# A routed feed-forward kernel: weight copies, the last weight split, the logits' update and the levels of the expert search put at other places in the schedule

## The chip, the cores and the metric

The kernel runs on one core of one Trainium2 chip. The metric is the device time of one execution in microseconds (us), taken as the median of several runs. The core has five engines that each work through their own instruction stream in order: TensorE (PE) for matrix products, VectorE (DVE), ScalarE (ACT), GpSimd (POOL) and SyncE (SP), which here only issues transfers. They wait for each other through semaphores.

## The reference

A gated linear attention produces 3072 rows of 384 numbers, and a mixture of 8 experts with a fixed capacity works on these rows. What is left of the second part when it is cut to what matters:

```python
logits = x @ w_gate                       # 3072 x 8
order = np.argsort(-logits.flatten())
for idx in order:                         # greedy, best score first
    tok, e = idx // E, idx % E
    if assigned[tok] >= 0 or counts[e] >= cap: continue      # cap = 384
    assigned[tok] = e; counts[e] += 1
for e in range(E):
    mask = assigned == e
    out[mask] = np.maximum(x[mask] @ w1[e], 0.0) @ w2[e]     # 384 -> 1024 -> 384
```

## The kernel before, in words

The first part of the span, up to about 150 us, computes the attention and the logits; nothing of it is touched. The rest treats the experts in the order in which they fill up, and does two things at once.

**The products.** For every expert, PE works through 8 blocks `q` of 128 hidden features. `ffn1(i, q)` (L818) is 9 matmuls into a PSUM tile `h`, of which there are two; ACT then writes `hh` (L823, the rounded ReLU) and DVE `hl` (L824, what the rounding left). `ffn2(i, q)` (L838) is 9 matmuls into `y`. Both use weights that are split into a rounded part and a residual: `split_hi` (L771, L772) is two copies on ACT into `whi`, `split_lo` (L780) two subtractions on POOL into `wlo`, so 16 subtractions `n` = 0 to 15 for an expert. The rows of the next expert are turned on PE (`rows`, L800), copied by ACT (`xh`, L801), and their residual `xl` is taken on DVE (`rows_lo`, L806). An expert has 144 product matmuls, and all 8 experts' products stand in one row, which sets the positions of everything else.

**The search.** While the products run, the kernel finds which expert fills up next and at which score. One search has five levels `t` = 0 to 4. Each level is a ring through two engines: PE counts (`counts`, L600, 24 small matmuls with the table `cmp` as weights), DVE compares with what room is left (`g`, L605), PE spreads that over the partitions (`flags`, L586, one matmul), DVE takes the level's digit (`k`, L588), the next digit (`nd`, L592) and builds the next table (`cmp`, L547), which the next level's counts wait for. After the fifth level `find` (L614 to L626) names the expert and starts the first half of its weights; `offsets` on PE and `places` on DVE (L644 to L675) give every chosen token its place, `one_hot` (L682, L684) turns the places into the tables `hot` and `rhs`, and PE multiplies them into a list of indices (`index`, L691). DVE copies it (`idx`, L696), POOL issues three gathers of the expert's rows (L698), and `best_left` (L720 to L735) strikes the full expert out of the logits `L`, takes every token's best score `m` that is left, and so begins the next search. The second half of the expert's weights is issued behind the gathers.

**What sets the order.** The order is written out by hand: `at(position, step)` puts a step before the product matmul of that number, and all instructions of a step go to the ends of their engines' streams at that moment. A loop over `i` places one search per round: round `i` holds the search for expert `i + 1` and the splits of expert `i`. A round's positions are counted from its `base`; `offs` holds the places of the five levels, `end` the place of the index matmuls, from which the next round's `base` follows. A step that has a small position difference to another leaves little time for the engines to go round. `BEHIND` gives for each of the 16 subtractions the level whose table must have been built first (0 to 4); this is an added wait on POOL, so that subtractions do not run while DVE builds a table.

In this text "search 2" is round `i` = 1 and "searches 3 to 6" are rounds 2 to 5, which have the same positions. Search 7 (round 6) is a shorter one. Expert 1's search lies in front of the loop, and is not touched.

Of the kernel before, what the change touches and what calls it, by code (L numbers as in the profile page):

```python
# [11 lines left out]
F16 = mybir.dt.float16  # L12
ROUTE_AHEAD = 3
LAST_BLOCKS = 2
BEHIND = (0, 0, 0, 1, 1, 2, 2, 3, 3, 4, 4, 4, 4, 4, 4, 4)
FREE_LAST = 4
WARM_UP = 10
Y_IN_LEVEL = (None, 11, 8, 8, 8)
# [8 lines left out]
OP = mybir.AluOpType  # L27
# [3 lines left out]
def gla_moe_kernel(ctx, tc, q, k, v, alpha, w_gate, w1, w2, out):  # L31
# [487 lines left out]
    def col(x, n=NU):  # L519
        return x[:, None, :].to_broadcast([128, n, x.shape[-1]])  # L520
# [157 lines left out]
    def one_hot(i):  # L678
        hot = st["hot"] = rw.tile([128, NW, T, U], F16, name="hot", bufs=1)
        rhs = st["rhs"] = rw.tile([128, NU, NB], F16, name="rhs")  # L680
        for a, js in enumerate(halves(i)):
            x = nc.vector.tensor_tensor(words(hot, T, js), keyed(st["wb"], T, js), each(iota, T, js), op=OP.is_equal)  # L682
            if a == 0:
                nc.vector.tensor_tensor(rhs, st["bk"], row(cst_c, NB), op=OP.mult)  # L684
        if i == E - 1:
            compared[i] = [None] * FREE_LAST + [x]

    def index(i):
        ix = psx.tile([128, NB], F32, name="xt")
# [27 lines left out]

    def best_left(i):
        es, v = st["es"], st["v"]
        nc.vector.scalar_tensor_tensor(L, col(cl_c), BIGNEG, L, op0=OP.mult, op1=OP.add)  # L720
        nc.vector.tensor_reduce(m_c, L, axis=X, op=OP.max)
        nc.vector.scalar_tensor_tensor(sel_c, v, float(CAP), qe_c, op0=OP.is_le, op1=OP.mult)
        val = st["val"] = rw.tile([128, NU, E], BF, name="val")
        if i + 2 < E:
# [50 lines left out]
    def split_lo(i, n):  # L775
        q, h = divmod(n, 2)
        if (i, q) not in CH:
            return False
        hi, lo, x = CH[i, q]
        y = nc.gpsimd.tensor_sub(lo[:, h], x[h], hi[:, h])  # L780
        if i + 1 in compared:
            after = compared[i + 1][BEHIND[n] if i + 2 < E else min(n, FREE_LAST)]
            if after is not None:
                tc.add_manual_dep(y.ins, after.ins.name,
                                  mybir.DependencyInfo(mybir.DependencyClass.Sync, mybir.DependencyReason.DATA),
                                  reason="weights split while the search reads one table at a time")
# [96 lines left out]
    def at(pos, fn, *args):  # L883
        plan.append((pos, len(plan), fn, args))
# [76 lines left out]
        at(p, split_lo, 0, n)  # L961
    base = 90
    for i in range(1, E):
        offs = dict(enumerate((36, 51, 65, 79, 93)))
        end = 140 if i == 1 else 144
        renewed(base, i) if i < E - 1 else at(base, gather, i)
        if i < E - 1:
            at(base + 9, new_choice, i)
        if i < E - 2:
            at(base + 14, table, i + 1, 0)  # L970
            at(base + 14, left, i)
        for b, p in enumerate((25, 34, 41) if i < E - 1 else (45, 60, 75)):
            at(base + p, rows, i, b)
        if i < E - 2:
            levels(base, i + 1, offs, {0: (0, 1), 1: (2,)})
            found(base + offs[4] + 3, i + 1, end - offs[4] - 3)
        else:
            for b, p in enumerate((29, 38, 45) if i < E - 1 else (49, 64, 79)):
                at(base + p, rows_lo, i, b)
        if i == E - 2:  # L980
            at(base + 12, find_last, i + 1)
# [3 lines left out]
            end = 58  # L985
            at(base + end, index, i + 1)
        if i < E - 2:
            hi = (24, 32, 50, 64, 86, 98, 108, 118)
            lo = (26, 26, 32, 55, 55, 71, 71, 87, 87, 103, 103, 103, 108, 108, 118, 118)
        elif i == E - 2:  # L990
            hi = (24, 32, 50, 64, 80, 96, 106, 118)
            lo = (26, 27, 32, 33, 50, 51, 64, 65, 80, 81, 96, 97, 106, 107, 118, 119)
        else:
            hi = [80 + 18 * q for q in range(5)] + [160, 170, 206]
            lo = [x for p in hi for x in (p, p + 1)]
# [70 lines left out]
```

## Time and profile before

| what | value |
|---|---|
| median of 3 runs (lowest, highest) | 425.96 us (425.06, 426.38) |
| the profiled execution's own time | 424.76 us |
| its span from first to last instruction | 423.1 us |
| mean granted clock of TensorE | 0.978 |
| PE busy | 394.1 us, 93% of the span |
| DVE busy | 288.8 us, 68% |
| POOL busy | 268.3 us, 63% |
| ACT busy | 194.0 us, 46% |
| bytes moved by DMA | 63.40 MB, mean 150 GB/s |

The durations in the prediction come from the profiled execution. Its time is 1.66 us more than its span, for what lies around it, and 1.20 us less than the median of the runs. PE is the engine that is nearly always busy, so the questions to put to this profile are where PE stands idle after the attention, for whom, and whether those waits go or come. A row of the timeline has the start and the duration in us, the engine, the line, the operation with its tiles, and in brackets how long the engine sat idle before it and who ended that. PE's matmuls overlap: the record of a product matmul is 0.33 us long, but the next one starts 0.17 us later. So what a wait costs PE is read from start to start.

### The profile page before, as it was taken

Reading aid. Unit: us, or ns where it says so; the run is one execution under the profiler, and the core shown is the slowest. Engines: PE = TensorE matmul, PEld = TensorE weight load, DVE = VectorE, ACT = ScalarE, POOL = GpSimd, SP = SyncE. Lnnn points to the kernel's source line nnn. Section 1 sums busy time; section 2 is a strip of 40 time slices with the busy share of each in tenths; the row PEclk is TensorE's granted clock in tenths of the full one; section 3 lists DMA queues with packets and bytes.
Section 4 is the critical chain, followed back from the end, with each engine's and each line's share of the span. In section 5 each row is a group of like instructions: output and inputs, shape, how many; then the busy total and the mean of one; then the engine's idle time right before and its main releaser. Section 6 shows DMA issues by size and latency. Waiting matters only on the chain.

```text
span 423.1 us, 10874 instructions
## 1 busy us (share of the span) xinstructions
PE 394.1 (93%) x4151; PEld 345.5 (82%) x4151; DVE 288.8 (68%) x836; ACT 194.0 (46%) x447; POOL 268.3 (63%) x327
## 2 busy tenths in 40 slices
PE   7999999889898958999999999999999999999993
PEld 3787777677676637998899899899899899999993
DVE  8888787888745686697697688589578677521220
ACT  2477566566575523425325325424343443654511
POOL 4668978677730026646566765665785775799932
PEclk9699999999999989999999999999999999999997
DMA  8999997670004577054055145155153333961011
GB/s 289 320 253 242 243 253 221 179 203 28 2 2 151 196 221 240 21 185 150 4 185 167 58 160 195 39 170 177 66 169 106 139 120 106 338 221 58 5 53 57
DMA packets 34884, 63.40 MB, mean 150 GB/s; under 512 B 3360, under 2 KB 15392, under 8 KB 34832
## 3 DMA queue, kind: packets, MB, share of 16 engines
q1 hardware_dynamic: 28592, 48.54, 37.9%
q0 software_dynamic: 3072, 9.44, 6.9%
q10 hardware_dynamic: 3168, 4.72, 3.2%
q8 instruction: 33, 0.54, 0.5%
q14 instruction: 19, 0.16, 0.1%
HBM read 53.25 MB, written 9.44 MB: 148 GB/s over the span
## 4 chain that ended last, share of the span: by engine, by line
PE 69%; DVE 17%; issue 4%; POOL 3%; ACT 3%; DMA 1%; DVEq 0%; ACTq 0%; POOLq 0%
PE y L838 18%; PE h L818 18%; PE rt L600 6%; PE y L314 5%; PE y L308 5%; PE s L259 5%; DVE hot L682 3%; DVE cmp L547 3%; PE xt L251 3%; POOL wlo L780 2%; PE st L327 2%; PE st L281 2%; DVE sc L222 2%; PE xt L691 2%; DVE ga L227 2%
## 5 line engine op out<-in xcount | busy, mean ns | idle before, releaser
L780 POOL TENSOR_TENSOR wlo<-w1r,whi 128x384 fp32r<-128x384 f32 x64 | 64.9, 1015 | 30.6 <-ACT whi L771 13.7
L823 ACT ACTIVATE hh<-h 128x384 fp32r<-128x384 f32 x64 | 31.5, 492 | 114.8 <-PE h L818 105.9
L780 POOL TENSOR_TENSOR wlo<-w2r,whi 128x384 fp32r<-128x384 f32 x64 | 66.4, 1037 | 20.7 <-DVE cmp L547 13.2
L824 DVE SCALAR_TENSOR_TENSOR hl<-h,hh 128x384 fp32r<-128x384 f32 x64 | 35.4, 553 | 46.8 <-ACT hh L823 45.7
L838 PE MATMUL y<-whi,hl 128*128 128x384 f32 x192 | 66.6, 347 | 0.0
L838 PE MATMUL y<-wlo,hh 128*128 128x384 f32 x192 | 65.8, 342 | 0.0
L838 PE MATMUL y<-whi,hh 128*128 128x384 f32 x192 | 65.3, 340 | 0.0
L698 POOL DMA_INDIRECT xr<-x_dram,idx x24 | 23.2, 966 | 51.4 <-DVE asg L728 29.3
L271 POOL TENSOR_SCALAR_AFFINE_SELECT sm<-sm 128x512 f32<-128x512 f32 x48 | 29.4, 639 | 31.5 <-ACT sm L267 31.5
L818 PE MATMUL h<-xh,whi 128*128 128x384 f32 x192 | 46.8, 344 | 0.4 <-ACT xh L801 0.3
L818 PE MATMUL h<-xh,wlo 128*128 128x384 f32 x192 | 45.8, 345 | 0.0
L818 PE MATMUL h<-xl,whi 128*128 128x384 f32 x192 | 45.8, 340 | 0.0
L292 ACT ACTIVATE sb<-st,sc 128x48 f32<-128x48 f32 x80 | 24.6, 331 | 35.8 <-DVE st L299 21.4
L838 PEld LDWEIGHTS y<-wlo,hh 128*128 128x128 f32 x192 | 36.2, 188 | 0.2
L838 PEld LDWEIGHTS y<-whi,hl 128*128 128x128 f32 x192 | 36.3, 189 | 0.0
L838 PEld LDWEIGHTS y<-whi,hh 128*128 128x128 f32 x192 | 36.1, 188 | 0.0
L771 ACT ACTIVATE whi<-w1r 128x384 fp32r<-128x384 f32 x64 | 33.1, 518 | 6.1 <-DMA w1r<-in_moe_w_dram 6.1
L547 DVE TENSOR_TENSOR cmp<-nd,iota 128x1536 bf16<-128x1536 bf16 (+7 forms) x32 | 34.6, 1092 | 1.0
L818 PEld LDWEIGHTS h<-xh,whi 128*128 128x128 f32 x192 | 33.9, 189 | 1.1 <-ACT xh L801 0.6
L855 POOL DMA_INDIRECT out_dram<-yt,idx x24 | 26.1, 1087 | 12.9 <-ACT yt L842 8.9
L818 PEld LDWEIGHTS h<-xl,whi 128*128 128x128 f32 x192 | 34.0, 188 | 0.0
L600 PEld LDWEIGHTS <-cmp 128*128 128x128 bf16 x720 | 26.3, 118 | 9.4 <-DVE cmp L547 6.6
(183 smaller groups left out, 817.4 us busy)
## 6 DMA issues: line engine op xcount, KB each, us to landing
w1r<-in_moe_w_dram SPq DMA_DIRECT2D x15, 768.0 KB, 4.7
w2r<-in_moe_w_dram SPq DMA_DIRECT2D x15, 768.0 KB, 6.2
vt<-in_v_dram SPq DMA_DIRECT2D x24, 256.0 KB, 6.0
x_dram<-xg ACTq DMA_DIRECT2D x6, 768.0 KB, 3.6
raw_a<-in_alpha_dram SPq DMA_DIRECT2D x19, 226.2 KB, 6.7
raw_k<-in_k_dram SPq DMA_DIRECT2D x19, 224.0 KB, 7.3
raw_q<-in_q_dram SPq DMA_DIRECT2D x19, 224.0 KB, 7.6
raw_a<-in_alpha_dram SPq DMA_DIRECT2D x5, 258.5 KB, 4.3
```

Of the source, the lines that this page charges most:

```text
L271: nc.gpsimd.affine_select(SM[s][:, h], SM[s][:, h], pattern=[[0, 4], [1, C]], compare_op=OP.is_ge, fill=0.0, base=0, channel_multiplier=-1)
L292: nc.scalar.activation(SB[s, u][:, :D], St[p], AF.Copy, scale=ac)
L547: x = nc.vector.tensor_tensor(words(dst, nt, js), keyed(d, nt, js), each(iotas[t], nt, js), op=OP.is_ge)
L600: nc.tensor.matmul(rt[:, 32:40], st["cmp"][:, j // U, :, j % U], st["o"][:, j], start=(j == 0), stop=(j == NU - 1))
L698: got = [nc.gpsimd.indirect_dma_start(out=XR[i][:, b], out_offset=None, in_=x_dram, in_offset=bass.IndirectOffsetOnAxis(ap=IDX[i][:, b:b + ...
L771: nc.scalar.activation(hi[:, 0], a, AF.Copy)
L780: y = nc.gpsimd.tensor_sub(lo[:, h], x[h], hi[:, h])
L818: nc.tensor.matmul(o, a[:, 0, d], x[:, d], start=(n == 0), stop=(n == 3 * DB - 1))
L823: nc.scalar.activation(hh, o, AF.Relu)
L824: nc.vector.scalar_tensor_tensor(hl, o, 0.0, hh, op0=OP.max, op1=OP.subtract)
L838: nc.tensor.matmul(Y[b], a[:, bs], w[:, 1].rearrange("p a b -> p (a b)"), start=(q == 0 and n == 0), stop=(q == FB - 1 and n == 2))
L855: st_ = nc.gpsimd.indirect_dma_start(out=out, out_offset=bass.IndirectOffsetOnAxis(ap=IDX[i][:, b:b + 1], axis=0), in_=yts.pop((i, b)), in ...
```

## The change

Only places in the schedule change, and one wait. No operation is added or taken away.

- **Copies sooner.** In rounds 1 to 5 the third to eighth `split_hi` move from positions 50, 64, 86, 98, 108, 118 to 48, 58, 70, 82, 92, 104, and the subtractions that follow them from 103 to 118 to 95 to 104.
- **The last split behind the one-hot.** Subtractions 14 and 15 move to position 126, behind `one_hot`, and `BEHIND` has 5 for them: they now wait for the table `hot` and not for the fifth level's. The list `compared` gets the one-hot's instruction for that.
- **The logits' update ahead of the indices.** The two instructions of the new function `without` (the update of `L` and the maximum) are issued right behind `one_hot` and no longer behind `idx`.
- **First counts ahead of the last residual.** In rounds 2 to 5 the first two `rows_lo` leave the first level and stand at 30 and 42, so the second of them, and the third, come behind that level.
- **New places for levels.** The levels stand at 36, 51, 65, 78, 92 in round 1 and at 34, 52, 65, 78, 92 in rounds 2 to 5 (before: 36, 51, 65, 79, 93 in all). Round 1 ends at 135 and no longer at 140, so that every later round begins 5 product matmuls sooner in the row of products. In rounds 2 to 5 `table` of the first level and `left` move from 14 to 19 and the second turn of rows from 34 to 38.

```diff
--- before.py
+++ after.py
@@ -12,7 +12,7 @@
 F16 = mybir.dt.float16
 ROUTE_AHEAD = 3
 LAST_BLOCKS = 2
-BEHIND = (0, 0, 0, 1, 1, 2, 2, 3, 3, 4, 4, 4, 4, 4, 4, 4)
+BEHIND = (0, 0, 0, 1, 1, 2, 2, 3, 3, 4, 4, 4, 4, 4, 5, 5)
 FREE_LAST = 4
 WARM_UP = 10
 Y_IN_LEVEL = (None, 11, 8, 8, 8)
@@ -682,8 +682,13 @@
             x = nc.vector.tensor_tensor(words(hot, T, js), keyed(st["wb"], T, js), each(iota, T, js), op=OP.is_equal)
             if a == 0:
                 nc.vector.tensor_tensor(rhs, st["bk"], row(cst_c, NB), op=OP.mult)
-        if i == E - 1:
-            compared[i] = [None] * FREE_LAST + [x]
+        compared[i] = [None] * FREE_LAST + [x] if i == E - 1 else compared.get(i, []) + [x]
+        if 0 < i < E - 1:
+            without(i)
+
+    def without(i):
+        nc.vector.scalar_tensor_tensor(L, col(cl_c), BIGNEG, L, op0=OP.mult, op1=OP.add)
+        nc.vector.tensor_reduce(m_c, L, axis=X, op=OP.max)
 
     def index(i):
         ix = psx.tile([128, NB], F32, name="xt")
@@ -717,8 +722,8 @@
 
     def best_left(i):
         es, v = st["es"], st["v"]
-        nc.vector.scalar_tensor_tensor(L, col(cl_c), BIGNEG, L, op0=OP.mult, op1=OP.add)
-        nc.vector.tensor_reduce(m_c, L, axis=X, op=OP.max)
+        if i == 0:
+            without(i)
         nc.vector.scalar_tensor_tensor(sel_c, v, float(CAP), qe_c, op0=OP.is_le, op1=OP.mult)
         val = st["val"] = rw.tile([128, NU, E], BF, name="val")
         if i + 2 < E:
@@ -779,7 +784,7 @@
         hi, lo, x = CH[i, q]
         y = nc.gpsimd.tensor_sub(lo[:, h], x[h], hi[:, h])
         if i + 1 in compared:
-            after = compared[i + 1][BEHIND[n] if i + 2 < E else min(n, FREE_LAST)]
+            after = compared[i + 1][min(BEHIND[n], len(compared[i + 1]) - 1) if i + 2 < E else min(n, FREE_LAST)]
             if after is not None:
                 tc.add_manual_dep(y.ins, after.ins.name,
                                   mybir.DependencyInfo(mybir.DependencyClass.Sync, mybir.DependencyReason.DATA),
@@ -961,21 +966,24 @@
         at(p, split_lo, 0, n)
     base = 90
     for i in range(1, E):
-        offs = dict(enumerate((36, 51, 65, 79, 93)))
-        end = 140 if i == 1 else 144
+        offs = dict(enumerate((36, 51, 65, 78, 92) if i == 1 else (34, 52, 65, 78, 92)))
+        end = 135 if i == 1 else 144
         renewed(base, i) if i < E - 1 else at(base, gather, i)
         if i < E - 1:
             at(base + 9, new_choice, i)
         if i < E - 2:
-            at(base + 14, table, i + 1, 0)
-            at(base + 14, left, i)
-        for b, p in enumerate((25, 34, 41) if i < E - 1 else (45, 60, 75)):
+            at(base + (14 if i == 1 else 19), table, i + 1, 0)
+            at(base + (14 if i == 1 else 19), left, i)
+        for b, p in enumerate((25, 34 if i == 1 else 38, 45) if i < E - 1 else (45, 60, 75)):
             at(base + p, rows, i, b)
         if i < E - 2:
-            levels(base, i + 1, offs, {0: (0, 1), 1: (2,)})
+            levels(base, i + 1, offs, {0: (0, 1), 1: (2,)} if i == 1 else {1: (2,)})
+            if i > 1:
+                at(base + 30, rows_lo, i, 0)
+                at(base + 42, rows_lo, i, 1)
             found(base + offs[4] + 3, i + 1, end - offs[4] - 3)
         else:
-            for b, p in enumerate((29, 38, 45) if i < E - 1 else (49, 64, 79)):
+            for b, p in enumerate((29, 38, 49) if i < E - 1 else (49, 64, 79)):
                 at(base + p, rows_lo, i, b)
         if i == E - 2:
             at(base + 12, find_last, i + 1)
@@ -985,8 +993,8 @@
             end = 58
             at(base + end, index, i + 1)
         if i < E - 2:
-            hi = (24, 32, 50, 64, 86, 98, 108, 118)
-            lo = (26, 26, 32, 55, 55, 71, 71, 87, 87, 103, 103, 103, 108, 108, 118, 118)
+            hi = (24, 32, 48, 58, 70, 82, 92, 104)
+            lo = (26, 26, 32, 55, 55, 71, 71, 87, 87, 95, 95, 96, 97, 104, 126, 126)
         elif i == E - 2:
             hi = (24, 32, 50, 64, 80, 96, 106, 118)
             lo = (26, 27, 32, 33, 50, 51, 64, 65, 80, 81, 96, 97, 106, 107, 118, 119)
```

Three places show what this does to the engines' streams. Line numbers of the changed kernel are 5 higher behind the new function, so `hl` is L824 before and L829 now.

On DVE, from level 2's counts to level 4's table in one of the searches 3 to 6 (`cmp_99` is the table of level 3, `cmp_98` with `iota_81` that of level 4), before:

```order
L605 TENSOR_TENSOR g<-rt,rem 128x8
L824 SCALAR_TENSOR_TENSOR hl<-h,hh 128x384
L588 TENSOR_REDUCE k<-rt 128x1
L592 SCALAR_TENSOR_TENSOR nd<-nd,k,scr 128x24
L547 TENSOR_TENSOR cmp_99<-nd,iota_80 128x6x256
L824 SCALAR_TENSOR_TENSOR hl<-h,hh 128x384
L605 TENSOR_TENSOR g<-rt,rem 128x8
L588 TENSOR_REDUCE k<-rt 128x1
L592 SCALAR_TENSOR_TENSOR nd<-nd,k,scr 128x24
L547 TENSOR_TENSOR cmp_98<-nd,iota_81 128x6x260
```

and now:

```order
L605 TENSOR_TENSOR g<-rt,rem 128x8
L588 TENSOR_REDUCE k<-rt 128x1
L592 SCALAR_TENSOR_TENSOR nd<-nd,k,scr 128x24
L547 TENSOR_TENSOR cmp_99<-nd,iota_80 128x6x256
L829 SCALAR_TENSOR_TENSOR hl<-h,hh 128x384
L605 TENSOR_TENSOR g<-rt,rem 128x8
L588 TENSOR_REDUCE k<-rt 128x1
L592 SCALAR_TENSOR_TENSOR nd<-nd,k,scr 128x24
L547 TENSOR_TENSOR cmp_98<-nd,iota_81 128x6x260
L829 SCALAR_TENSOR_TENSOR hl<-h,hh 128x384 x2
```

The `hl` that stood between `g` and `k` ahead of level 3's table stands behind that table now.

On DVE around the one-hot of the same search (`bk` is the last instruction of `places`; `idx` copies what PE's index matmuls made of `hot` and `rhs`), before:

```order
L675 TENSOR_TENSOR bk<-scr,bsel 128x72
L824 SCALAR_TENSOR_TENSOR hl<-h,hh 128x384
L682 TENSOR_TENSOR hot<-wb,iota 128x3072
L684 TENSOR_TENSOR rhs<-bk,scr 128x72
L824 SCALAR_TENSOR_TENSOR hl<-h,hh 128x384
L711 TENSOR_SCALAR oh<-pcs,k 65x1
L696 TENSOR_SCALAR idx<-xt 128x3
L720 SCALAR_TENSOR_TENSOR L<-scr,L 128x192
L721 TENSOR_REDUCE scr<-L 128x24
```

and now:

```order
L675 TENSOR_TENSOR bk<-scr,bsel 128x72
L682 TENSOR_TENSOR hot<-wb,iota 128x3072
L684 TENSOR_TENSOR rhs<-bk,scr 128x72
L690 SCALAR_TENSOR_TENSOR L<-scr,L 128x192
L691 TENSOR_REDUCE scr<-L 128x24
L829 SCALAR_TENSOR_TENSOR hl<-h,hh 128x384 x2
L716 TENSOR_SCALAR oh<-pcs,k 65x1
L701 TENSOR_SCALAR idx<-xt 128x3
```

No `hl` stands between `bk` and `hot` any more, and two of them and the logits' update stand between `rhs` and `idx`.

On ACT, from the output tiles `yt` of the expert before to the last copies of a round's split, before:

```order
L842 ACTIVATE yt<-y_3883 128x384
L771 ACTIVATE whi<-w1r 128x384
L772 ACTIVATE whi<-w2r 128x384
L823 ACTIVATE hh<-h 128x384 x3
L771 ACTIVATE whi<-w1r 128x384
L772 ACTIVATE whi<-w2r 128x384
L771 ACTIVATE whi<-w1r 128x384
L772 ACTIVATE whi<-w2r 128x384
L823 ACTIVATE hh<-h 128x384
```

and now:

```order
L847 ACTIVATE yt<-y_3895 128x384
L776 ACTIVATE whi<-w1r 128x384
L777 ACTIVATE whi<-w2r 128x384
L828 ACTIVATE hh<-h 128x384 x2
L776 ACTIVATE whi<-w1r 128x384
L777 ACTIVATE whi<-w2r 128x384
L828 ACTIVATE hh<-h 128x384
L776 ACTIVATE whi<-w1r 128x384
L777 ACTIVATE whi<-w2r 128x384
L776 ACTIVATE whi<-w1r 128x384
L777 ACTIVATE whi<-w2r 128x384
```

The fifth split's copies stood behind three `hh` and stand right behind `yt` now; the others follow sooner too. POOL's stream has the same instructions in the same order as before. SP's stream differs at one place: the first half of expert 7's weights now stands ahead of the second half of expert 6's.

## The prediction

> **What bounds the kernel now.** I read the page first, then the windows of four searches and of the end, then PE's waits, then the timelines of PE, DVE and POOL. Each engine's busy time:
>
> ```profile
> PE 394.1 (93%) x4151; PEld 345.5 (82%) x4151; DVE 288.8 (68%) x836; ACT 194.0 (46%) x447; POOL 268.3 (63%) x327
> ```
>
> Stages, from one index product to the next (the first and the last of searches 3 to 6, which repeat each other), and the end; PE's busy time stands first:
>
> ```profile
> 217.40:251.20 33.80, 33.11 (x307) 30.83 (x308) 25.70 (x74) 13.39 (x30) 22.29 (x25) 1.00 0.39 129
> ...
> 318.70:352.40 33.70, 33.01 (x307) 30.73 (x308) 25.66 (x74) 13.39 (x30) 22.32 (x25) 1.00 0.38 130
> 352.40:416.00 63.60, 63.59 (x393) 62.80 (x391) 19.70 (x51) 28.64 (x64) 47.62 (x59) 1.00 0.35 122
> ```
>
> A search leaves PE 0.69 us idle of some 33.7; behind the last search PE never stops, at clock 1.00. So the most that an order can win here is PE's waits in the searches, and a wait won there moves the end by as much. Who is waited for (total, times, longest):
>
> ```profile
> PE xt L691 <- DVE rhs L684: 5.1, 6, 3.2
> ...
> PE rt L600 <- DVE cmp L547: 3.5, 7, 1.0
> ...
> PE xt L800 <- DMA xr<-x_dram,idx: 0.4, 1, 0.4
> ```
>
> DVE's one-hot and tables end PE's waits. PE's timeline, mostly search 5 (bracket: idle before, releaser):
>
> ```profile
> 205.66 0.68 PE L818 MATMUL h<-xh,whi 128*128 128x384 f32 x3
> 207.02 0.96 PE L600 MATMUL rt<-o,cmp 128*128 128x8 bf16 x24 [0.68 <-DVE cmp L547]
> 293.17 0.34 PE L838 MATMUL y<-whi,hh 128*128 128x384 f32 x1
> 293.48 0.17 PE L586 MATMUL rt<-g,one 128*128 128x8 bf16 x1
> 299.53 0.34 PE L818 MATMUL h<-xl,whi 128*128 128x384 f32 x1
> 299.71 0.96 PE L600 MATMUL rt<-o,cmp 128*128 128x8 bf16 x24
> 300.53 0.60 PE L818 MATMUL h<-xl,whi 128*128 128x384 f32 x2
> 302.16 0.68 PE L818 MATMUL h<-xl,whi 128*128 128x384 f32 x3
> 302.68 0.68 PE L818 MATMUL h<-xh,whi 128*128 128x384 f32 x3
> 303.64 0.96 PE L600 MATMUL rt<-o,cmp 128*128 128x8 bf16 x24 [0.28 <-DVE cmp L547]
> 317.01 0.34 PE L838 MATMUL y<-wlo,hh 128*128 128x384 f32 x1
> 317.76 0.93 PE L691 MATMUL xt<-rhs,hot 128*128 128x3 f16 x24 [0.41 <-DVE rhs L684]
> ```
>
> Product matmuls start 0.173 apart (302.16 to 302.68 for three), and without a wait the counts follow 0.18 behind one (299.53 to 299.71). Start to start, search 5 loses: at the index product 0.75 - 0.18 = 0.57; at level 3's counts 303.64 - 303.03 (the third matmul of its row) - 0.18 = 0.43; at the first flags 0.31 - 0.18 = 0.13. That is 1.13. Search 2 loses 207.02 - 206.01 - 0.18 = 0.83 at level 4's counts.
>
> **The change part by part.** Why those waits are there, on DVE (the first row is an undisturbed one-hot, the second a disturbed table of level 4):
>
> ```profile
> 181.59 1.75 DVE L682 TENSOR_TENSOR hot<-wb,iota 128x3072 f16<-128x3072 bf16 x1
> 205.61 1.36 DVE L547 TENSOR_TENSOR cmp<-nd,iota 128x1560 bf16<-128x1560 bf16 x1
> 298.18 0.96 DVE L547 TENSOR_TENSOR cmp<-nd,iota 128x1536 bf16<-128x1536 bf16 x1
> 301.69 0.56 DVE L824 SCALAR_TENSOR_TENSOR hl<-h,hh 128x384 fp32r<-128x384 f32 x1 [0.81 <-ACT hh L823]
> 302.63 0.96 DVE L547 TENSOR_TENSOR cmp<-nd,iota 128x1536 bf16<-128x1536 bf16 x1
> 305.13 0.17 DVE L588 TENSOR_REDUCE k<-rt 128x1 f32<-128x8 f32 x1 [0.32 <-PE rt L586]
> 305.61 0.97 DVE L547 TENSOR_TENSOR cmp<-nd,iota 128x1560 bf16<-128x1560 bf16 x1
> 313.08 0.22 DVE L675 TENSOR_TENSOR bk<-scr,bsel 128x72 f16<-128x72 int32 x1
> 313.92 0.56 DVE L824 SCALAR_TENSOR_TENSOR hl<-h,hh 128x384 fp32r<-128x384 f32 x1 [0.62 <-ACT hh L823]
> 314.40 3.17 DVE L682 TENSOR_TENSOR hot<-wb,iota 128x3072 f16<-128x3072 bf16 x1
> ```
>
> and on POOL:
>
> ```profile
> 205.13 1.01 POOL L780 TENSOR_TENSOR wlo<-w1r,whi 128x384 fp32r<-128x384 f32 x1 [1.84 <-ACT whi L771]
> 298.46 1.56 POOL L855 DMA_INDIRECT out_dram<-yt,idx  x1 [0.16 <-issue]
> 301.02 1.03 POOL L780 TENSOR_TENSOR wlo<-w1r,whi 128x384 fp32r<-128x384 f32 x1
> 302.25 1.01 POOL L855 DMA_INDIRECT out_dram<-yt,idx  x1 [0.19 <-issue]
> 313.98 1.00 POOL L780 TENSOR_TENSOR wlo<-w1r,whi 128x384 fp32r<-128x384 f32 x1
> 314.95 1.00 POOL L780 TENSOR_TENSOR wlo<-w2r,whi 128x384 fp32r<-128x384 f32 x1
> ```
>
> *The one-hot.* It took 3.17 beside two subtractions and 1.75 free: 1.42 lost. Those two wait for it now. The `hl` ahead of it, which waited for `hh`, goes too: `hot` started 1.32 behind `bk` and can start some 0.2 behind it. That is 2.5 us sooner, less about 0.95 that DVE now waits in front of `places` for another `hl`, since the level stands 6 positions nearer to that product. The wait was 0.57, so it goes with about 1 us to spare: 4 x 0.57 = 2.3. What queues behind the waiting subtractions on POOL is the three gathers, which need the indices anyway; the two end 2.0 us behind the one-hot, before `idx`.
>
> *Levels.* From counts to the next table's start DVE needs 305.61 - 303.64 = 1.97, and from there to the next counts 303.64 - 302.63 = 1.01: 2.98 undisturbed. PE needs 303.64 - 0.43 - 299.71 = 3.50 for 14 positions, so 3.33 for 13. With no `hl` between `g` and `k` the wait at level 3 (0.43) and, in search 2, at level 4 (0.83) goes. From level 0 to level 1, 18 positions, an `hl` stands in the ring now. PE needs 18 x 0.173 + 1.07 (what the 3.50 hold beside 14 positions) + two turns of rows,
>
> ```profile
> 289.64 0.33 PE xt L800 x3
> ```
>
> so 4.85. On DVE the `hl` starts 0.9 behind its product's last matmul (300.79, the second of its row, to 301.69), which is 1.1 behind the counts' start; `hl` to `k` 0.47, `k` to table 0.48, the wide table 1.75: 4.7. I take nothing; a miss of 0.2 would cost 0.8 in all.
>
> *First counts ahead of the residual.* `g` no longer waits behind two `xl`; the 0.13 at the flags goes.
>
> The sum of what goes: 4 x 1.13 + 0.83 = 5.35.
>
> *What comes: tables beside subtractions.* A table that met a subtraction begun 0.48 earlier (205.13 and 205.61) took 1.36 for 0.96, 0.40 lost. POOL's sixth and seventh subtraction follow level 2's table at fixed distance: the seventh runs from 301.02 - 298.18 = 2.84 to 3.87 behind its start. Level 3's table started 4.45 behind it and now, at 13 positions and without `hl`, 3.33 behind: it meets that subtraction for 0.54. Loss 0.40 against 3.33 - 2.98 = 0.35 to spare: 0.05. Level 4's table starts 6.71 behind. The scatter between takes 1.01 (302.25), or 1.56 when it starts inside a table's build (298.46), as it now does. With 1.01 the ninth subtraction, whose copies are there sooner, runs from 6.07 to 7.05, the loss of 0.34 is within the 0.52 to spare; with 1.56 it starts at 6.62, about 0.8 is lost, and PE waits 0.26. I take the middle, 0.13. Together 0.18 a search, 0.7 in four; bounds 0.2 to 1.2.
>
> On descriptors the Trainium skill differs from that row: "SBUF — State Buffer", section "Who interferes with whom", infers that a two-input DVE operation leaves GpSimd's descriptor writing alone, as it takes only the shared read interface. By it the scatter would take 1.01, and the sum would be 0.5 us better than mine; the row of 1.56 beside a `tensor_tensor` speaks against it.
>
> *Copies sooner.* The fifth split's copies stand behind `yt` and the fourth's. Issue and landing of the weights' second half, and `yt`:
>
> ```profile
> 291.60 0.37 SPq L533 DMA_DIRECT2D w2r<-in_moe_w_dram  x1
> ```
>
> ```profile
> DMA to landing us min/median/max: 4.0/6.1/8.5
> ```
>
> ```profile
> 298.15 1.03 ACT L842 ACTIVATE yt<-y 128x384 f32<-128x384 f32 x2 [0.16 <-PE y L838]
> ```
>
> It lands at 297.7 by the median and at 300.1 by the longest; the copies come at 299.2 + 0.8 = 300.0 at the earliest. No wait. The swap on SP (expert 7's first half ahead of expert 6's second) delays the latter by about the 4.5 between the shortest and the longest landing, where ACT needs it 16 us behind the index: nothing.
>
> *Logits' update.* Two `hl` and the update now stand ahead of `idx`, and one `hl` comes from the product right in front of the index matmuls; I count 0.3 us later gathers. PE waited for gathered rows once (0.4, the first expert), so I take nothing; bound 4 x 0.3. The update itself, two instructions of about 0.4, leaves the path behind `idx`, which makes level 0's table sooner; that has room.
>
> Net: 5.35 - 0.7 = 4.6. For the profiled execution 424.76 becomes 420.1, its span 418.5; it lies 1.20 under the median, so on the median's scale **421.3**.
>
> **The rivals.**
>
> *All waits go and none comes* (18%): POOL's copies arrive so that no table meets a subtraction. 425.96 - 5.35 = 420.6. For it: undisturbed rings have 0.35 to spare. Against: the 3.33 falls into the seventh subtraction.
>
> *A table waits for the whole subtraction* (17%): then level 3 loses 0.54 (0.19 at PE) and level 4, with the long scatter, 0.75 (0.23): 0.42 x 4 = 1.7 back, 422.3. For it: the one-hot, which lost about as long as POOL worked. Against: the row at 205.61, where 0.53 of overlap cost 0.40. The skill's same section states this rule: whoever issues first holds the shared pair for the whole instruction.
>
> *The waits move* (13%): `hh` behind sooner copies, or the level 0 ring, gives back the 1.13 of each search; only search 2 gains: 425.1. Against: ACT is busy 13.4 of 33.7.
>
> *Slower* (7%): levels 3 and 4 each meet two subtractions in a row, as the one-hot did, and lose 1.42: 1.07 and 0.90 at PE, 7.9 in four searches, 425.96 - 5.35 + 7.9 = 428.5. It decides from 1.34 a search on. For it: sooner copies take away POOL's pause at 303 to 307, which kept level 4's table free. Against: a scatter stands behind the seventh subtraction.
>
> **How the numbers follow.** The forecast has 45%: 421.3, its own range 420.9 to 422.0. Faster are forecast, first and second rival: 80%; within 0.3%, about what a measurement of this kernel can tell from no change, is the third: 13%; slower 7%. The range 420.0 to 424.9 leaves out the slower case and most of the third; its low end is the first rival less 0.6 for the runs' scatter.
>
> **What would show it.** The waits view should lose nearly all of `xt` L691 but the first 3.2, and have `rt` L600 only with small times; the one-hot of searches 2 to 6 should take 1.75. Level 3's table should take about 1.36, level 4's up to 1.8. Index products of searches 3 to 6 should stand about 32.8 apart (33.75 before). I am wrong if PE waits for `h` or `y` operands, or if one-hots stay above 2.

## The result, and the profile after

The changed kernel takes **422.10 us** (median of 20 runs, 420.98 to 427.65), the kernel before 425.97 us beside it (median of 20, 424.85 to 431.32). The ratio is 0.9906, with a 95% interval of 0.9887 to 0.9925: faster by 0.9%, 3.9 us. The forecast was 421.3 with a range of 420.0 to 424.9, so it had the side and the range, and promised 0.8 us too much. The forecast's own range, 420.9 to 422.0, was missed by 0.1, and the second rival's 422.3 was nearer than the forecast.

The profiled execution of the changed kernel took 422.51 us, its span is 420.8. That span is only 2.3 us shorter than the one before. The rest of the gain is hidden by 1.6 us that lie ahead of everything that was changed: the first expert's index product starts at 152.95 instead of 151.35. So the comparison below starts behind that point. From the start of the index product of expert 1's search to the start of PE's last matmul, 232.1 us became 228.3 (183.53 to 415.65 before, 185.11 to 413.41 after): 3.8 us, as in the medians.

The page's busy times after:

```profile
PE 395.1 (94%) x4151; PEld 346.4 (82%) x4151; DVE 285.9 (68%) x836; ACT 194.0 (46%) x447; POOL 271.1 (64%) x327
```

DVE works 2.9 us less and POOL 2.8 us more, though neither was given other work: operations that meet got longer or shorter. Searches 3 and 6 from one index product to the next, and the end (windows; length, then PE's busy time first, DVE's third, POOL's fifth):

```profile
217.17:250.18 33.01, 32.94 (x307) 30.71 (x307) 25.14 (x75) 13.38 (x30) 24.38 (x27) 1.00 0.41 133
316.30:349.36 33.06, 32.99 (x307) 30.74 (x308) 25.15 (x75) 13.39 (x30) 23.45 (x25) 1.00 0.40 133
349.36:413.80 64.44, 64.39 (x396) 63.55 (x396) 19.61 (x51) 28.82 (x65) 47.63 (x60) 1.00 0.36 120
```

A search fell from 33.7 or 33.8 to 33.0 or 33.1. PE's idle time in it fell from 0.69 to 0.07 us by this view; what is lost between the starts of its matmuls is not all in it. PE's waits (total, times, longest):

```profile
PE xt L696 <- DVE rhs L684: 3.4, 2, 3.2
...
PE rt L600 <- DVE cmp L547: 1.6, 2, 0.9
```

Before, these two entries were 5.1 and 3.5. What is left of them lies ahead of the loop, up to the search of expert 1, which is not touched. PE's timeline in search 5, with the rows that answer to the waits of before (the last row has 20 of the 24 index matmuls, where the view ends):

```profile
289.52 0.34 PE L823 MATMUL h<-xl,whi 128*128 128x384 f32 x1
289.80 0.93 PE L600 MATMUL rt<-o,cmp 128*128 128x8 bf16 x24
...
300.72 0.69 PE L823 MATMUL h<-xh,wlo 128*128 128x384 f32 x3
301.32 0.96 PE L600 MATMUL rt<-o,cmp 128*128 128x8 bf16 x24
304.64 0.34 PE L843 MATMUL y<-wlo,hh 128*128 128x384 f32 x1
305.06 0.96 PE L600 MATMUL rt<-o,cmp 128*128 128x8 bf16 x24
...
314.79 0.68 PE L823 MATMUL h<-xl,whi 128*128 128x384 f32 x3
315.31 0.83 PE L696 MATMUL xt<-rhs,hot 128*128 128x3 f16 x20
```

None of these rows carries a bracket any more, but three of them still lose a little from start to start, beyond the 0.18 of an unhindered step: level 0's counts 289.80 - 289.52 - 0.18 = 0.10 (0.11 with the trace's third digit), level 3's 301.32 - 301.06 (the third matmul of its row, at steps of 0.17) - 0.18 = 0.08, level 4's 305.06 - 304.64 - 0.18 = 0.24. The index product loses nothing. DVE's timeline says why:

```profile
287.29 0.56 DVE L829 SCALAR_TENSOR_TENSOR hl<-h,hh 128x384 fp32r<-128x384 f32 x1 [0.26 <-issue]
287.76 1.75 DVE L547 TENSOR_TENSOR cmp<-top,iota 128x3072 bf16<-128x3072 bf16 x1
...
289.59 0.15 DVE L761 TENSOR_TENSOR rem<-rem,rt 128x8 f32<-128x8 f32 x1
...
296.57 0.96 DVE L547 TENSOR_TENSOR cmp<-nd,iota 128x1536 bf16<-128x1536 bf16 x1
...
299.89 1.38 DVE L547 TENSOR_TENSOR cmp<-nd,iota 128x1536 bf16<-128x1536 bf16 x1
...
303.29 1.71 DVE L547 TENSOR_TENSOR cmp<-nd,iota 128x1560 bf16<-128x1560 bf16 x1
...
306.06 0.17 DVE L605 TENSOR_TENSOR g<-rt,rem 128x8 bf16<-128x8 f32 x1
...
309.63 0.56 DVE L829 SCALAR_TENSOR_TENSOR hl<-h,hh 128x384 fp32r<-128x384 f32 x1 [0.97 <-ACT hh L828]
...
312.06 0.22 DVE L675 TENSOR_TENSOR bk<-scr,bsel 128x72 f16<-128x72 int32 x1
312.20 1.75 DVE L682 TENSOR_TENSOR hot<-wb,iota 128x3072 f16<-128x3072 bf16 x1
```

and POOL's, in the same search:

```profile
296.76 1.66 POOL L860 DMA_INDIRECT out_dram<-yt,idx  x1 [0.16 <-issue]
...
299.41 1.03 POOL L785 TENSOR_TENSOR wlo<-w1r,whi 128x384 fp32r<-128x384 f32 x1
...
300.64 1.51 POOL L860 DMA_INDIRECT out_dram<-yt,idx  x1 [0.18 <-issue]
...
303.15 1.01 POOL L785 TENSOR_TENSOR wlo<-w1r,whi 128x384 fp32r<-128x384 f32 x1
...
304.35 1.51 POOL L860 DMA_INDIRECT out_dram<-yt,idx  x1 [0.16 <-issue]
```

The one-hot is free (1.75) and follows `bk` at once. Level 3's table (299.89) meets the seventh subtraction (299.41) and takes 1.38; level 4's (303.29) meets the ninth (303.15) and takes 1.71. The scatters, which begin within a table, take 1.51 to 1.66. Level 0's table starts behind an `hl` that sat idle 0.26 until `hh` was there, at 287.25 by ACT's timeline:

```profile
286.76 0.49 ACT L828 ACTIVATE hh<-h 128x384 fp32r<-128x384 f32 x1 [3.79 <-PE h L823]
```

That table is nevertheless in time by itself. The tables of levels 3 and 4 end 0.05 and 0.06 ahead of their counts (301.27 and 305.00); level 0's ends at 289.51, and PE was ready at 289.52 + 0.18 = 289.70. What ends 0.06 ahead of level 0's counts is `rem` (289.59 + 0.15 = 289.74), which DVE does behind the table, and which reads the tile `rt` that the counts write. So the wait there is for `rem`; the bracket in the kernel "old update" below names it too. No run moves `rem` alone.

So three small losses stand where the rings and the one-hot lost more before.

### The profile page after: what moved, and what is told of

The parts are those of the page before. It is cut to its first block, busy times and chain, and to the rows that moved or that the text cites. A ratio compares the mean times of both kernels' runs of the same rounds, so it can differ in the third digit from the quotient of the medians.

```text
span 420.8 us, 10878 instructions
## 1 busy us (share of the span) xinstructions
PE 395.1 (94%) x4151; PEld 346.4 (82%) x4151; DVE 285.9 (68%) x836; ACT 194.0 (46%) x447; POOL 271.1 (64%) x327
## 4 chain that ended last, share of the span: by engine, by line
PE 68%; DVE 15%; POOL 6%; issue 5%; DMA 2%; ACT 2%; SPq 0%; ACTq 0%; DVEq 0%; POOLq 0%
PE y L843 19%; PE h L823 19%; PE rt L600 6%; PE y L314 5%; PE y L308 4%; PE s L259 4%; DVE cmp L547 3%; POOL wlo L785 3%; DVE ga L227 2%; PE xt L251 2%; DVE sc L222 2%; POOL out_dram L860 2%; PE xt L696 2%; PE st L327 2%; PE st L281 2%
## 5 line engine op out<-in xcount | busy, mean ns | idle before, releaser
L785 POOL TENSOR_TENSOR wlo<-w2r,whi 128x384 fp32r<-128x384 f32 x64 | 65.0, 1016 | 20.2 <-ACT whi L776 7.6
L829 DVE SCALAR_TENSOR_TENSOR hl<-h,hh 128x384 fp32r<-128x384 f32 x64 | 35.1, 553 | 50.0 <-ACT hh L828 43.1
L843 PE MATMUL y<-whi,hh 128*128 128x384 f32 x192 | 66.8, 348 | 0.0
L271 POOL TENSOR_SCALAR_AFFINE_SELECT sm<-sm 128x512 f32<-128x512 f32 x48 | 29.3, 635 | 33.1 <-ACT sm L267 33.1
L823 PE MATMUL h<-xh,wlo 128*128 128x384 f32 x192 | 44.9, 339 | 0.0
L860 POOL DMA_INDIRECT out_dram<-yt,idx x24 | 30.6, 1273 | 13.9 <-ACT yt L847 9.8
L547 DVE TENSOR_TENSOR cmp<-nd,iota 128x1536 bf16<-128x1536 bf16 (+7 forms) x32 | 37.6, 1185 | 1.0
L823 PEld LDWEIGHTS h<-xh,wlo 128*128 128x128 f32 x192 | 34.1, 188 | 0.0
```

Source lines behind the costliest of these rows:

```text
L271: nc.gpsimd.affine_select(SM[s][:, h], SM[s][:, h], pattern=[[0, 4], [1, C]], compare_op=OP.is_ge, fill=0.0, base=0, channel_multiplier=-1)
L547: x = nc.vector.tensor_tensor(words(dst, nt, js), keyed(d, nt, js), each(iotas[t], nt, js), op=OP.is_ge)
L823: nc.tensor.matmul(o, a[:, 0, d], x[:, d], start=(n == 0), stop=(n == 3 * DB - 1))
L829: nc.vector.scalar_tensor_tensor(hl, o, 0.0, hh, op0=OP.max, op1=OP.subtract)
L843: nc.tensor.matmul(Y[b], a[:, bs], w[:, 1].rearrange("p a b -> p (a b)"), start=(q == 0 and n == 0), stop=(q == FB - 1 and n == 2))
L860: st_ = nc.gpsimd.indirect_dma_start(out=out, out_offset=bass.IndirectOffsetOnAxis(ap=IDX[i][:, b:b + 1], axis=0), in_=yts.pop((i, b)), in ...
```

## The experiments

Two theories stood against each other for the gain: that each edit wins the wait it was worked out for (the one-hot by the last split, levels 3 and 4 by the places), or that it came from somewhere else in the schedule. For the 0.8 us that were missing, theory one was the meeting of POOL's subtractions with the tables; its rival was that a ring of 13 positions has no room, whatever POOL does.

Times of one kernel scatter by more than most of these edits are worth, so beside the medians stands a distance from one profiled execution each: from the start of the index product of search 2 to that of search 6, which holds searches 3 to 6.

| kernel | median, us | ratio to before, 95% interval | index products of searches 2 and 6 | distance |
|---|---|---|---|---|
| before | 425.97 | | 216.43, 351.52 | 135.09 |
| changed | 422.10 | 0.9906, 0.9887 to 0.9925 | 216.19, 348.38 | 132.19 |
| split alone | 424.33 | 0.9990, 0.9954 to 1.0027 | 216.61, 349.53 | 132.92 |
| split free | 422.33 | 0.9924, 0.9878 to 0.9971 | 221.08, 353.29 | 132.21 |
| free tables | 420.90 | 0.9876, 0.9834 to 0.9919 | 216.14, 347.03 | 130.89 |
| free tables, sooner table 0 | 420.58 | 0.9866, 0.9827 to 0.9906 | 216.21, 346.81 | 130.60 |
| round 1 ends at 140 | 422.85 | 0.9914, 0.9885 to 0.9943 | 216.29, 349.36 | 133.07 |
| level 4 free | 420.53 | 0.9857, 0.9828 to 0.9885 | 215.41, 346.64 | 131.23 |
| old update | 424.39 | 0.9961, 0.9932 to 0.9990 | 218.00, 351.98 | 133.98 |
| old copies | 424.46 | 0.9974, 0.9926 to 1.0023 | 215.92, 350.57 | 134.65 |
| old copies, scatter later | 420.69 | 0.9860, 0.9793 to 0.9926 | 215.28, 346.50 | 131.22 |
| old copies, fifth sooner | 422.17 | 0.9919, 0.9878 to 0.9959 | 215.20, 347.42 | 132.22 |

**Split alone.** The kernel before, with the wait for the one-hot and nothing else:

```diff
-BEHIND = (0, 0, 0, 1, 1, 2, 2, 3, 3, 4, 4, 4, 4, 4, 4, 4)
+BEHIND = (0, 0, 0, 1, 1, 2, 2, 3, 3, 4, 4, 4, 4, 4, 5, 5)
...
-            lo = (26, 26, 32, 55, 55, 71, 71, 87, 87, 103, 103, 103, 108, 108, 118, 118)
+            lo = (26, 26, 32, 55, 55, 71, 71, 87, 87, 103, 103, 103, 108, 108, 126, 126)
```

> The kernel before with one edit alone: the last two subtractions wait for the one-hot. Theory (each edit wins the wait that it was worked out for): the one-hots of searches 2 to 6 take 1.75, the wait in front of the index product goes, 0.57 in each of searches 3 to 6, 2.3 in all: 423.7, index products of searches 3 to 6 about 33.2 apart instead of 33.75. Rival (the one-hot is held by the hl ahead of it, or the two subtractions behind it make the gathers late): no more than 0.5 is won, 425.5 or above.

DVE's timeline of this kernel in search 5:

```profile
312.18 0.22 DVE L675 TENSOR_TENSOR bk<-scr,bsel 128x72 f16<-128x72 int32 x1
313.03 0.56 DVE L823 SCALAR_TENSOR_TENSOR hl<-h,hh 128x384 fp32r<-128x384 f32 x1 [0.63 <-ACT hh L822]
313.51 1.75 DVE L682 TENSOR_TENSOR hot<-wb,iota 128x3072 f16<-128x3072 bf16 x1
```

The one-hot takes 1.75, although the `hl` still stands ahead of it. The four searches shrank by 135.09 - 132.92 = 2.17; 2.3 were expected. The times by themselves decide nothing here: their interval reaches from 0.9954 to 1.0027. The trace bears the theory out: this edit alone wins more than half of what the whole change wins.

**Split free.** The changed kernel without that wait; the last two subtractions follow the fourteenth:

```diff
-BEHIND = (0, 0, 0, 1, 1, 2, 2, 3, 3, 4, 4, 4, 4, 4, 5, 5)
+BEHIND = (0, 0, 0, 1, 1, 2, 2, 3, 3, 4, 4, 4, 4, 4, 4, 4)
...
-            lo = (26, 26, 32, 55, 55, 71, 71, 87, 87, 95, 95, 96, 97, 104, 126, 126)
+            lo = (26, 26, 32, 55, 55, 71, 71, 87, 87, 95, 95, 96, 97, 104, 104, 104)
```

> The changed kernel, but the last two subtractions do not wait for the one-hot: they follow the fourteenth at once. Theory (a DVE operation stands still until the subtraction that it meets is over, and does its whole work behind it): the sooner copies alone already end the last subtraction at about 312.7 where the one-hot starts at 312.2; it takes 2.2 to 2.3, ends some 0.4 later, and the index product, which follows the one-hot by 1.4, does not wait: 422.1, and the gathers start sooner. Rival (the one-hot is held for more than the overlap, as beside two subtractions, 3.17): PE waits some 0.2 to 0.3 in each of four searches, 423 or above.

DVE's one-hot and the last subtraction on POOL in search 5:

```profile
317.10 2.13 DVE L682 TENSOR_TENSOR hot<-wb,iota 128x3072 f16<-128x3072 bf16 x1
```

```profile
316.61 1.00 POOL L785 TENSOR_TENSOR wlo<-w2r,whi 128x384 fp32r<-128x384 f32 x1
321.95 0.98 POOL L703 DMA_INDIRECT xr<-x_dram,idx  x1 [4.34 <-DVE scr L727]
```

The one-hot loses 0.38 for an overlap of 317.61 - 317.10 = 0.51, and the distance is the changed kernel's (132.21 and 132.19; this kernel's profiled execution is some 5 us later, which it was already at the index product of expert 1's search, 190.01 against 185.11). So the wait for the one-hot, which wins 2.2 us in the kernel before, wins nothing here: with sooner copies POOL's last subtraction ends early enough that the one-hot's loss of 0.38 costs PE nothing. One part of the expectation failed: the gathers do not start sooner (1.74 behind the index product in both), because they wait for `idx`.

**Round 1 ends at 140.** On top of the kernel "free tables, sooner table 0" below, one number as before:

```diff
-        end = 135 if i == 1 else 144
+        end = 140 if i == 1 else 144
```

> The kernel with free tables and the sooner table of level 0, and one number back as before: round 1 ends at 140 and not at 135, so that the levels of searches 3 to 6 stand at the same places of a round, but 5 product matmuls later in the row of products. Theory (what the new places won is that no hl falls into the rings of levels 3 and 4): an hl stands again between level 2's g and k; with 13 positions its counts at level 3 lose 0.43 + 0.17 = 0.60, level 0's table has an hl ahead of it again, 0.11, and index products of searches 3 to 6 stand about 33.35 apart instead of 32.65: 2.8 more, 423.4. Rival (the smaller distances of the levels and the residual behind the first counts won it, wherever a product ends): 32.65 apart, 420.6.

DVE's timeline of search 5 in this kernel, from level 2's `g`, and PE's at level 3's counts:

```profile
299.41 0.17 DVE L605 TENSOR_TENSOR g<-rt,rem 128x8 bf16<-128x8 f32 x1 [1.39 <-PE rt L600]
300.39 0.56 DVE L829 SCALAR_TENSOR_TENSOR hl<-h,hh 128x384 fp32r<-128x384 f32 x1 [0.81 <-ACT hh L828]
300.87 0.16 DVE L588 TENSOR_REDUCE k<-rt 128x1 f32<-128x8 f32 x1
```

```profile
301.38 0.51 PE L823 MATMUL h<-xh,whi 128*128 128x384 f32 x2
302.35 0.96 PE L600 MATMUL rt<-o,cmp 128*128 128x8 bf16 x24 [0.46 <-DVE cmp L547]
```

The `hl` is back between `g` and `k`, and level 3's counts lose 302.35 - 301.55 - 0.18 = 0.62 (0.60 expected). The distance grows by 2.47, the median by 2.3. So it was not the smaller distance between levels that won level 3's wait, but where the products end: five product matmuls decide whether an `hl` falls into the ring. Level 0 lost nothing, 0.11 were expected there.

**Level 4 free.** The changed kernel with one number changed, so that the ninth subtraction waits for level 4's table:

```diff
-BEHIND = (0, 0, 0, 1, 1, 2, 2, 3, 3, 4, 4, 4, 4, 4, 5, 5)
+BEHIND = (0, 0, 0, 1, 1, 2, 2, 3, 4, 4, 4, 4, 4, 4, 5, 5)
```

> The changed kernel with one number changed: the ninth subtraction waits for level 4's table and not for level 3's. Theory (each table's loss stands by itself): level 4's table takes 0.97 and its counts lose nothing, level 3's still takes 1.38 and its counts lose 0.08; index products of searches 3 to 6 stand 32.81 apart instead of 33.05, the time is 1.0 less, 421.1. Rival (the waits of levels 3 and 4 are linked through POOL's order, so that one alone only moves): 33.0 apart.

DVE's tables of levels 3 and 4 in search 5:

```profile
298.64 1.38 DVE L547 TENSOR_TENSOR cmp<-nd,iota 128x1536 bf16<-128x1536 bf16 x1
...
302.04 0.97 DVE L547 TENSOR_TENSOR cmp<-nd,iota 128x1560 bf16<-128x1560 bf16 x1
```

Level 4's is free, level 3's is not, and the distance falls by 0.96, 0.24 a search: as the theory had it.

**Free tables**, all three subtractions that meet these two tables moved behind them, and **sooner table 0**:

```diff
-BEHIND = (0, 0, 0, 1, 1, 2, 2, 3, 3, 4, 4, 4, 4, 4, 5, 5)
+BEHIND = (0, 0, 0, 1, 1, 2, 3, 4, 4, 4, 4, 4, 4, 4, 5, 5)
```

> The changed kernel with three subtractions of a round waiting for a later table: the seventh for level 3's, the eighth and ninth for level 4's, so that no subtraction runs beside these two tables. Theory (PE's new waits of 0.08 at level 3 and 0.24 at level 4 are the subtractions' doing): both tables of searches 3 to 6 take 0.96 again, both waits go, 0.32 in each of four searches, 1.3 us: 420.8. Rival A (the ring at 13 positions has no room, whatever POOL does): tables 0.96, but the same time, 422.1. Rival B (POOL, some 1.6 us later, runs into the one-hot and is late with the residuals): 422.1 or slower, with the index product waiting or PE waiting for wlo.

```diff
-            at(base + (14 if i == 1 else 19), table, i + 1, 0)
+            at(base + 14, table, i + 1, 0)
```

> The same as the kernel with free tables, and level 0's table of searches 3 to 6 ahead of the hl in front of it (position 14 and not 19; the second of DVE's two steps there stays at 19). Theory (level 0's counts lose 0.11 a search since that hl waits for hh): 0.44 us less than the kernel with free tables, 420.4. Rival (the loss at level 0 is made good at level 1, whose ring has only 0.1 to spare and now starts sooner): the same time as the kernel with free tables.

Three groups of DVE in the kernel with free tables (mean ns of one behind the bar and the busy time):

```profile
L682 DVE TENSOR_TENSOR hot<-wb,iota 128x3072 f16<-128x3072 bf16 x7 | 14.0, 2005 | 0.0
L547 DVE TENSOR_TENSOR cmp<-nd,iota 128x1536 bf16<-128x1536 bf16 x12 | 11.5, 957 | 0.4
...
L547 DVE TENSOR_TENSOR cmp<-nd,iota 128x1560 bf16<-128x1560 bf16 x6 | 5.8, 972 | 0.2
```

and the same groups in the changed kernel:

```profile
L547 DVE TENSOR_TENSOR cmp<-nd,iota 128x1536 bf16<-128x1536 bf16 x12 | 13.2, 1098 | 0.4
L682 DVE TENSOR_TENSOR hot<-wb,iota 128x3072 f16<-128x3072 bf16 x7 | 12.2, 1748 | 0.0
...
L547 DVE TENSOR_TENSOR cmp<-nd,iota 128x1560 bf16<-128x1560 bf16 x6 | 8.8, 1460 | 0.2
```

The tables are free, and the distance falls by 1.30 (0.33 a search, 0.32 expected), the median to 420.90. Rival A, the ring without room, is out. Of rival B a part came true: POOL, now later, runs its fourteenth subtraction into the one-hot, which takes 2.2 in searches 3 to 6; that costs PE nothing, for the reason seen in the split-free kernel. The sooner table 0 takes another 0.29 (0.07 a search, 0.11 expected). With 420.58 us, ratio 0.9866 (0.9827 to 0.9906), this kernel is the fastest by the trace; by the times alone it can't be told from the kernels with 420.5 to 420.9.

**Old update.** The changed kernel with `without` behind `idx` again:

```diff
-        if 0 < i < E - 1:
-            without(i)
...
-        if i == 0:
-            without(i)
+        without(i)
```

> The changed kernel with the logits' update back behind idx. Theory (level 0's table of searches 3 to 6 already ends 0.11 later than PE comes to its counts, so that DVE's chain behind idx ends PE's wait there): the two instructions, 0.35 and 0.36 with some 0.03 between, put that table 0.74 later, level 0's counts wait 0.85 in place of 0.11, index products of searches 3 to 6 stand 33.8 apart instead of 33.05, and the time is 3.0 longer, 425.1. Rival (what the prediction said: level 0's table has room): 33.05 apart, 422.1.

PE's counts of level 0 in search 5 of this kernel (the first 17 of the 24, where the view ends), and DVE's rows ahead of them:

```profile
292.94 0.70 PE L600 MATMUL rt<-o,cmp 128*128 128x8 bf16 x17 [0.38 <-DVE rem L758]
```

```profile
290.16 0.36 DVE L752 TENSOR_TENSOR o<-scr,chu 128x192 bf16<-128x192 f32 x1
290.44 0.55 DVE L826 SCALAR_TENSOR_TENSOR hl<-h,hh 128x384 fp32r<-128x384 f32 x1
290.90 1.75 DVE L547 TENSOR_TENSOR cmp<-top,iota 128x3072 bf16<-128x3072 bf16 x1
```

The direction is the theory's and the size is not: 1.79 more over the four searches, 0.45 each, where 0.74 was expected. The `hl` ahead of the table follows `o` at once here; in the changed kernel it sat 0.26 waiting for `hh`, which swallows that much of the two instructions. The prediction's "that has room" fails for the level: moving the update was worth about 0.45 a search at the level's new place.

**Old copies.** The changed kernel with the copies of before:

```diff
-            hi = (24, 32, 48, 58, 70, 82, 92, 104)
-            lo = (26, 26, 32, 55, 55, 71, 71, 87, 87, 95, 95, 96, 97, 104, 126, 126)
+            hi = (24, 32, 50, 64, 86, 98, 108, 118)
+            lo = (26, 26, 32, 55, 55, 71, 71, 87, 87, 103, 103, 103, 108, 108, 126, 126)
```

> The changed kernel with the weight copies of the third to eighth split at the positions of before, and the subtractions 9 to 13 at theirs; the last two still wait for the one-hot. Theory (sooner copies won nothing by themselves and let the ninth subtraction run into level 4's table): that table takes 0.97, its counts do not wait 0.24, index products of searches 3 to 6 stand 32.8 apart instead of 33.05: 1.0 less, 421.1. Rival (sooner copies are needed so that the fourteenth subtraction is over ahead of the one-hot): the one-hot takes over 3 and the index product waits, 33.1 apart or more.

DVE, POOL and PE of this kernel in search 5:

```profile
304.26 0.97 DVE L547 TENSOR_TENSOR cmp<-nd,iota 128x1560 bf16<-128x1560 bf16 x1
...
307.62 0.17 DVE L605 TENSOR_TENSOR g<-rt,rem 128x8 bf16<-128x8 f32 x1 [0.90 <-PE y L843]
```

```profile
306.30 0.99 POOL L860 DMA_INDIRECT out_dram<-yt,idx  x1 [0.15 <-issue]
```

```profile
305.79 0.96 PE L600 MATMUL rt<-o,cmp 128*128 128x8 bf16 x24
...
307.91 0.17 PE L586 MATMUL rt<-g,one 128*128 128x8 bf16 x1 [0.70 <-DVE cs L583]
```

Theory and rival both failed. Level 4's table is free (0.97) and the one-hot too (1.75), as the theory said and the rival didn't; but the kernel is slower, 134.65 against 132.19. That is 33.66 a search, the rival's number without its reason. A new wait took the place: `g` starts 307.62 - 305.79 = 1.83 behind its counts' start, where it is 306.06 - 305.06 = 1.00 in the changed kernel, and PE waits for it. The two kernels have the same instructions in the same order on DVE and PE there, and the matmuls of the counts took no longer; PE's signal that they were done (its semaphore update) came late. ACT's copies begin at the same distances behind level 4's table in both kernels (0.18 and 1.77 for the first and third). What was different at that moment was POOL: a scatter ran across the end of the counts. The next two kernels ask whether that is it.

**Old copies, scatter later**, and **old copies, fifth sooner**:

```diff
-            for b, p in enumerate((56, 72, 88)):
+            for b, p in enumerate((56, 72, 104 if i < E - 2 else 88)):
```

> The kernel with the old copies, and the third scatter of rounds 2 to 5 at position 104 and not at 88, so that POOL issues it behind the twelfth subtraction. There PE's signal that level 4's counts are done came 1.02 to 1.05 behind the start of the last of the 24 matmuls, where it comes 0.19 behind it in every other level of every trace, while POOL wrote that scatter's descriptors (306.30 to 307.29). Theory (it is that scatter): the signal comes after 0.19 again, the 0.86 in front of level 4's flags goes, index products of searches 3 to 6 stand 32.8 apart instead of 33.65: 421.1. Rival (it is not the scatter; ACT's later copies or something that no row shows): 33.65 apart, 424.5.

```diff
-            hi = (24, 32, 50, 64, 86, 98, 108, 118)
+            hi = (24, 32, 50, 64, 70, 98, 108, 118)
```

> The kernel with the old copies, and one of them at the changed place: the fifth split's two copies at position 70 and not at 86. Theory (of the copies' places only this one matters to PE, since the ninth subtraction, and the scatter behind it, follow it): the ninth subtraction runs into level 4's table again, which takes 1.7, the scatter again ends ahead of the counts, and index products of searches 3 to 6 stand 33.05 apart as in the changed kernel: 422.1. Rival (the copies of the later splits, behind position 86, hold PE's signal or hh): the 0.86 in front of level 4's flags stays, 33.65 apart or more.

Both came out as the theory had them. With the scatter elsewhere the old copies are as good as the kernel "level 4 free" (131.22 and 131.23). With only the fifth split's copies sooner, the distance is 132.22, as in the changed kernel. So the sooner copies as such are worth nothing to PE in the new places; one of the six decides when POOL does its ninth subtraction and the scatter behind it. That PE's signal is late with this scatter there, and in time with it elsewhere, is shown. How the one delays the other isn't: other scatters were running while PE's signals came in time (in the kernel with free tables 0.45 and 0.75 behind a scatter's start).

## Why the prediction was right, and where it missed

- **Waits that go.** The index product (0.57), level 3's counts (0.43) and the first flags (0.13) no longer lose this: 1.13 a search, as forecast. Search 2 won more than its 0.83: it took 32.90 before and 31.08 after, of which 5 product matmuls (0.87) only belong to the next round now, so 0.95.
- **Why they go.** The one-hot (1.75, `hl` behind another operation, 0.97 waited ahead of `places` for 0.95 forecast) and the `hl` out of the rings were shown one by one, by the split alone and by the round that ends at 140. The ring from level 0 to level 1, forecast at 4.7 against 4.85, costs nothing. The prediction did not see that the sooner copies alone would have saved the index product: without the added wait the distance is the same (132.21). The flags' 0.13 and search 2's part are read from the traces alone and have no run of their own, nor has the third turn of rows, which the diff moves from 41 to 45 and the list of changes leaves out.
- **What comes: the term that was mis-sized.** Forecast were 0.05 at level 3 and 0.13 at level 4, 0.7 us in all; measured 0.08 and 0.24, 1.3 us. The durations were foreseen (1.36 and up to 1.8; they are 1.38 and 1.71). What failed is "I take the middle, 0.13": the text had said that the scatter starts inside a table's build, where the one row of the profile had it at 1.56, and then gave half weight to a scatter of 1.01. It took 1.51 in each of searches 3 to 6.
- **The rule of the Trainium skill that was weighed against that row.** "SBUF — State Buffer", section "Who interferes with whom", infers that a two-input DVE operation leaves descriptor writing alone. The scatters that begin within a table took 1.51 to 1.66, and those that begin outside one 0.99 to 1.01 in the experiments' rows (the profile page's group of all 24 scatters grew from a mean of 1087 ns to 1273): the measurement decides against it. That section of the Trainium skill also has the rule that the second to issue waits for the whole instruction, which is borne out here but for some 0.13 us. Level 3's table ends 301.27, 0.83 behind the end of the seventh subtraction, and level 4's 305.00, 0.84 behind the ninth's; a free table takes 0.96. The row that the prediction set against this rival fits as well: the table at 205.61 ended 0.83 behind the subtraction's end (206.97 and 206.14). In all four meetings read here, with overlaps of 0.53, 0.55, 0.87 and (at the one-hot of the split-free kernel) 0.51, the loss was the overlap less 0.13: 0.40, 0.42, 0.74 and 0.38.
- **The second rival**, which had that rule, named 0.19 and 0.23 at PE for the two levels and a time of 422.3. Its sum was nearer than the forecast's: level 4 is as it said, level 3 came 0.11 lower, and the 0.11 of level 0, which nobody had, made up for that; that part was luck.
- **The logits' update and level 0.** "That has room" was wrong: 0.11 a search is lost at level 0, 0.4 us in all, and it would be 0.45 more without the move. The table itself had 0.13 to spare (289.70 - 289.51 - 0.06), `rem` behind it had none. In the kernel before, 22 positions lie between that table's place and its counts (14 and 36), in the changed kernel 15 (19 and 34), and the prediction did not work the difference out.
- **Copies sooner** were costed at nothing by their landing, which holds. That they set when POOL's ninth subtraction and third scatter run was seen only as a cost at level 4.

Each of the four searches won 1.13 and lost 0.11 + 0.08 + 0.24 = 0.43 again, a net of 0.70; measured is (135.09 - 132.19) / 4 = 0.72. So index products stand 33.05 apart, and not 32.8 as the prediction's signs had it. With search 2's 0.95 the measured sum is 2.90 + 0.95 = 3.85. The medians differ by 3.87; that these agree so closely is chance, since the runs of one kernel scatter by more.

## What to carry to other kernels

Where one row shows that an operation is long when it starts beside another engine's, take the long value for every place where your own arithmetic puts it there, and no middle. Before adding a wait that keeps two engines apart, see whether the order of the other work already does: of two edits that each cure the same meeting, the second is worth nothing. And when an off-path engine's work is moved, follow it to the next two things in its queue, since here the places of one copy and one scatter decided through POOL whether a search took 32.8, 33.05 or 33.66 us.

## What the runs showed of the hardware

- A scatter on POOL that begins within a table's build behaves as if it could not get on until the table is done: the three of search 5 end 0.86 to 0.89 behind the end of the table they began in (298.42 behind 297.53, 302.15 behind 301.27, 305.86 behind 305.00). In the twelve traces all 88 that begin within a table take 1.50 to 1.67, the other 200 0.97 to 1.02. The table itself is not longer for it (296.57: 0.96). A scatter that begins 0.38 ahead of a table loses nothing: before, one ran 1.01 from 302.25 and the table in it took 0.96 from 302.63.
- In one order, and in each of its four equal searches, PE's signal for the end of the counts came 1.02 to 1.05 behind the start of the last matmul, with a scatter running, and not 0.19 as in all other levels of the twelve traces. It cost 0.86 a search. The cause within the chip stays open.
